# Down layer of the first chunk in fp32, bonus of the second chunk by feature, heads 6/7 of two units by a 0/1 matrix, last down layer by halves

## The chip, the core and the metric

The kernel runs on one core of a Trainium2 chip. The metric is the device time of one execution in microseconds. The engines are TensorE (PE), VectorE (DVE), ScalarE (ACT), GpSimd (POOL) and SyncE (SP), which issues all DMAs here.

## What is computed

A linear attention with decay runs over 4 batches, 8 heads, 768 steps and 48 features; its output of 3072 tokens of 384 features goes through two feed-forward layers. The first takes the largest of three projections and projects down; the second is a gated one. The host of the kernel gives the weights as 64-bit floats.

```python
for t in range(S):
    kt, vt, rt, wt = (k[:, :, t], v[:, :, t], r[:, :, t], w[:, :, t])
    cur = np.einsum('bhd,bhe->bhde', u[None] * kt, vt)
    y[:, :, t] = np.einsum('bhd,bhde->bhe', rt, state + cur)
    state = wt[:, :, :, None] * state + np.einsum('bhd,bhe->bhde', kt, vt)
# first layer, 384 -> 768 -> 384
h = np.maximum(np.maximum(x @ w1, x @ w2), x @ w3);  x = h @ w_out
# second layer, 384 -> 1536 -> 384
g = x @ w_gate;  out = (g * (1.0 / (1.0 + np.exp(-g))) * (x @ w_val)) @ w_out2
```

## The kernel before

**Chunks and units.** The 768 steps are cut into six chunks c = 0 to 5 of 128 steps; a chunk holds 512 tokens (4 batches), which are the columns of its matrices. A chunk's attention is made in four units j, in the order 3, 0, 1, 2, numbered n = 0 to 23 through the kernel. Unit j = 3 makes heads 6 and 7, units 0, 1, 2 two heads each. The matrix x of a chunk has three tiles of 128 rows (k = 0, 1, 2, one for each of units 0, 1, 2): 48 rows of a head, 16 rows of heads 6/7, the same again. The 16-row pieces are copied by small DMAs from the tile of unit 3 (`xsh`, `xsl`) into the tiles of the others (`gather`, L556).

**A unit.** DVE makes a scan of the decays from the end (`suffix`, L358), its product with k (`khats`, L363), a scan from the start (`prefix`, L371) and its product with r (`rps`, L374). PE makes transposes (L461), k-v products (`outer`, L516), scores (L447). The bonus u*r*k stands on the diagonal of the score matrix A: ACT writes A with the bonus (`diag`, L439), DVE masks the scores into it (`causal`, L452). PE adds A times v (`intra`, L476, two halves with a short ACT read, `peek`, between) and the state's part (`inter`, L489) into one PSUM tile `y`. The bonus is made in two ways: in the first chunk DVE multiplies r by k by feature (`rk`, L418), PE sums by u (`rk_sum`, L424), ACT copies (L431); in the others a second copy of r and k, with tokens on partitions (`inpT`, 384 KB), is loaded, POOL multiplies it (`bonus`, L406/407) and DVE sums (`bonus_sum`, L411).

**Two parts.** The large matmuls are made in fp32r with three products: a matrix is an upper part (`hi`, `xh`, `hh`: a copy to fp32r) and a lower part (`lo`, `xl`, `hl`: the rest), and `mm3` (L566 to 569) multiplies upper by upper, upper by lower, lower by upper. So each x, each hidden matrix and each weight needs an ACT copy (`upper` L534, `hidden` L631, `whigh` L596) and a DVE subtraction (`lower` L554, `hidden` L634, `wlow` L599). In the first chunk the lower part of x is made otherwise: PE subtracts the upper part in PSUM by a matrix -1 (`take_upper`, L543), ACT copies the rest (L552). Before that a weight is put together from its 64-bit words by three DVE steps (`f64_bits`, L128 to 130). Weights 0 to 5 are the up weights, 6 and 7 the two halves of the down weights, 8 to 19 those of the second layer.

**First layer.** For each chunk 18 groups `up` (f, m) of nine matmuls of 512 columns, the largest of three m by ACT (m = 0, L624) and DVE (L626), two parts of it; then `down` (m, k) for m = 0, 1, 2 and halves k = 0, 1 of the six f, nine matmuls each. The results go to DRAM (`y1d`). Units of the next chunk are threaded between the groups. After the last unit (`second_half`, L723) the attention's memory is given to the second layer: 72 groups of 27 matmuls.

**Order.** All steps are entered in a table with an engine, a cost, what they wait for and a due time; `Plan.order` (L59) makes the static order of each engine from it. Four PSUM slots (`slot`) are shared by the groups of large matmuls, the transposes, `outer` and the bonus sums; `y` has one tile, which is free when the lower part of the unit before is made.

Of the kernel before, what the change touches and what calls it, by code (L numbers as in the profile page):

```python
# [124 lines left out]
def f64_bits(nc, lw, hw, tmp):  # L125


    yield nc.vector.tensor_scalar(tmp, hw, 3, 0x3FFFFFFF, ALU.logical_shift_left, ALU.bitwise_and)  # L128
    yield nc.vector.scalar_tensor_tensor(lw, lw, 29, tmp, ALU.logical_shift_right, ALU.bitwise_or)
    yield nc.vector.scalar_tensor_tensor(lw, hw, -0x40000000, lw, ALU.bitwise_and, ALU.bitwise_or)  # L130


def f64_general(nc, pool, dst, src):

    n = dst.shape[1]
    for o in range(0, n, 384):
# [5 lines left out]
        list(f64_bits(nc, lw, hw, d.bitcast(I32)))  # L142
# [129 lines left out]
def fused(ctx: ExitStack, tc: tile.TileContext, pk, ub, wt_all, out):  # L272
    nc = tc.nc
    units = [(c, j) for c in range(NC_) for j in ORDER]

# [25 lines left out]
    minus = ap.tile([128, 128], F32R, name="minus")  # L301
    inpA = [ap.tile([128, OFF_KT], F32, name=f"inpA{i}") for i in range(2)]
# [130 lines left out]
    def diag(n, half):  # L433
# [33 lines left out]

    def intra(n, k):

        for b in range(2):  # L470
            for h in range(2):
                for s in range(2):
# [4 lines left out]
                        ys[n][64 * h:64 * h + 64, a, C * b + T * s:C * b + T * s + T],  # L477
                        inpV[n][t, D * i:D * i + 64], A[n][t, i, :],
                        start=(k == 1 and b == 0), stop=True, skip_group_check=True,
# [15 lines left out]
    def first_y(n):  # L495
        ys[n] = psA.tile([128, 2, NT], F32, tag="y", name="y")
        intra(n, 1)
# [87 lines left out]
    def bits(i, k):  # L585

        if k == 0:
            tmp = lp.tile([128, WCH], I32, tag="tmp", name="tmp")
            ops[i] = f64_bits(nc, raws[i][:, :, 0], raws[i][:, :, 1], tmp)
        next(ops[i], None)  # L590

# [29 lines left out]
    def up_out(c, f, m):  # L621
        if m == 0:
# [13 lines left out]
    def down(c, m, k):  # L636
# [3 lines left out]
        for f in range(3 * k, 3 * k + 3):  # L640
            mm3(pss[c, m], hi[6 + k][:, f % 3, q], lo[6 + k][:, f % 3, q], hh[f], hl[f], f == 0, f == 5)
# [114 lines left out]
    for turn, what in enumerate(chunks):  # L756
# [32 lines left out]
        for k in range(3):  # L789
            cost = 0.67 if k == 0 else 1.28  # L790
            war = [L["bits", i - 1, 1]] if k == 0 and ("bits", i - 1, 1) in L else []
            b = L["bits", i, k] = on("DVE", cost, bits, i, k)([ld if k == 0 else b] + war)
        h = L["high", i] = on("ACT", 1.16, whigh, i)([b])
        l = L["low", i] = on("DVE", 1.28, wlow, i)([h], need)
        users[turn] = [l]
# [11 lines left out]
    for n, (c, j) in enumerate(units):  # L807
# [3 lines left out]
        due = 10 + 6.0 * i if early else START[c - 1] + (i + 1) * (PERIOD / 4) - 18  # L811
# [26 lines left out]
        tr = L["tr", n] = on("PE", 0.45, transposes, n)([kh] + prev("outer", n, 1), slot=1, slack=lag)  # L838
# [229 lines left out]
```

## Time and profile before

| | us |
|---|---|
| median of 3 runs (lowest to highest) | 879.13 (878.44 to 879.92) |
| the profiled execution | 879.41 |
| its span, first to last instruction | 877.5 |
| PE busy | 844.8 (96%) |
| DVE busy | 437.5 (50%) |
| ACT busy | 342.5 (39%) |
| POOL busy | 91.1 (10%) |
| mean granted clock of TensorE | 0.982 |

Busy time is a sum over the whole span, and the span has stages with different limits, so the page's strips of 40 slices and tables by stage come first. Matmuls are pipelined: the record of one with 512 columns is 0.39 us long while the next starts 0.23 us later, so a busy PE can still be late. A granted clock of 1.00 is 2.4 GHz, 0.50 is 1.2 GHz. In the first 27 us the column shows 1.00 though the durations of matmuls there are those of the stretches at 0.50.

### The profile page before, as it was taken

Reading aid. Unit: us, or ns where it says so; the run is one execution under the profiler, and the core shown is the slowest. Engines: PE = TensorE matmul, PEld = TensorE weight load, DVE = VectorE, ACT = ScalarE, POOL = GpSimd, SP = SyncE. Lnnn points to the kernel's source line nnn. Section 1 sums busy time; section 2 is a strip of 40 time slices with the busy share of each in tenths; the row PEclk is TensorE's granted clock in tenths of the full one; section 3 lists DMA queues with packets and bytes.
Section 4 is the critical chain, followed back from the end, with each engine's and each line's share of the span. In section 5 each row is a group of like instructions: output and inputs, shape, how many; then the busy total and the mean of one; then the engine's idle time right before and its main releaser. Section 6 shows DMA issues by size and latency. Waiting matters only on the chain.

```text
span 877.5 us, 15085 instructions
## 1 busy us (share of the span) xinstructions
PE 844.8 (96%) x6322; PEld 682.9 (78%) x6322; DVE 437.5 (50%) x626; ACT 342.5 (39%) x721; POOL 91.1 (10%) x116
## 2 busy tenths in 40 slices
PE   6797899999999999989999999999999999999997
PEld 5675677787777778768788888888888888888885
DVE  6999997745665657369884212222222212222221
ACT  4644455655354454455555221232132122222111
POOL 1422133111211100010100100010010010000000
PEclk9699999999999999999999999999999999999999
DMA  8775476355433553154731100020010000000001
GB/s 235 193 211 190 146 226 166 75 171 139 130 94 111 149 133 118 47 186 147 245 112 51 36 37 1 0 72 1 1 36 37 1 13 36 1 1 37 0 1 39
DMA packets 24635, 79.54 MB, mean 91 GB/s; under 512 B 4016, under 2 KB 7216, under 8 KB 20976
## 3 DMA queue, kind: packets, MB, share of 16 engines
q1 hardware_dynamic: 24560, 78.50, 30.0%
q8 instruction: 51, 0.84, 0.4%
q14 instruction: 24, 0.20, 0.1%
HBM read 66.69 MB, written 9.44 MB: 87 GB/s over the span
## 4 chain that ended last, share of the span: by engine, by line
PE 83%; DVE 9%; DMA 4%; ACT 2%; issue 1%; SPq 1%; DVEq 0%
PE ps L567 9%; PE ps L568 9%; PE ps L569 8%; PE po L567 6%; PE po L568 6%; PE pg L568 6%; PE pv L568 6%; PE pg L567 6%; PE pv L567 6%; PE po L569 6%; PE pg L569 6%; PE pv L569 6%; PE y L476 2%; PE sc L447 1%; PE kv L516 1%
## 5 line engine op out<-in xcount | busy, mean ns | idle before, releaser
L696 DVE TENSOR_TENSOR sil<-sil,pv 128x512 f32<-128x512 f32 x72 | 49.4, 686 | 252.1 <-PE pv L569 250.0
L567 PE MATMUL ps<-xh,hi 128*128 128x512 f32 x324 | 133.5, 412 | 4.4 <-DMA xh<-xsh 2.5
L569 PE MATMUL ps<-xh,lo 128*128 128x512 f32 x324 | 129.0, 398 | 1.5 <-DVE lo L599 1.5
L568 PE MATMUL ps<-xl,hi 128*128 128x512 f32 x324 | 128.9, 398 | 1.2 <-DMA xl<-xsl 1.2
L693 ACT ACTIVATE sil<-pg 128x512 f32<-128x512 f32 x72 | 42.9, 596 | 162.3 <-PE pg L569 162.3
L700 ACT ACTIVATE ph<-sil 128x512 fp32r<-128x512 f32 x72 | 45.4, 630 | 126.1 <-DVE sil L696 126.1
L568 PE MATMUL po<-pl,hi 128*128 128x512 f32 x216 | 84.6, 392 | 0.0
L568 PE MATMUL pg<-yl,hi 128*128 128x512 f32 x216 | 84.6, 392 | 0.0
L568 PE MATMUL pv<-yl,hi 128*128 128x512 f32 x216 | 84.6, 392 | 0.0
L567 PE MATMUL po<-ph,hi 128*128 128x512 f32 x216 | 84.5, 391 | 0.0
L567 PE MATMUL pg<-yh,hi 128*128 128x512 f32 x216 | 84.4, 391 | 0.0
L567 PE MATMUL pv<-yh,hi 128*128 128x512 f32 x216 | 84.3, 390 | 0.0
L569 PE MATMUL po<-ph,lo 128*128 128x512 f32 x216 | 83.9, 389 | 0.0
L569 PE MATMUL pg<-yh,lo 128*128 128x512 f32 x216 | 83.9, 389 | 0.0
L569 PE MATMUL pv<-yh,lo 128*128 128x512 f32 x216 | 83.9, 388 | 0.0
L705 DVE TENSOR_TENSOR pl<-sil,ph 128x512 fp32r<-128x512 f32 x72 | 49.8, 691 | 56.7 <-ACT ph L700 56.7
L567 PEld LDWEIGHTS ps<-xh,hi 128*128 128x128 f32 x324 | 62.1, 192 | 20.1 <-issue 2.9
L569 PEld LDWEIGHTS ps<-xh,lo 128*128 128x128 f32 x324 | 62.0, 191 | 16.3 <-DVE lo L599 2.9
L568 PEld LDWEIGHTS ps<-xl,hi 128*128 128x128 f32 x324 | 62.2, 192 | 13.7 <-issue 2.1
L626 DVE TENSOR_TENSOR hw<-hw,ps 128x512 f32<-128x512 f32 x72 | 49.0, 681 | 43.1 <-PE ps L569 36.2
L681 POOL TENSOR_TENSOR yl<-y,yh 128x512 fp32r<-128x512 f32 x18 | 24.2, 1348 | 348.4 <-ACT yh L677 348.4
L439 ACT ACTIVATE A<-stacked,a 128x64 f32<-128x64 f32 x192 | 49.5, 336 | 9.0 <-DVE a L411 8.8
(111 smaller groups left out, 1353.3 us busy)
## 6 DMA issues: line engine op xcount, KB each, us to landing
raw<-wt SPq DMA_DIRECT2D x28, 1152.0 KB, 6.1
inpA<-pk SPq DMA_DIRECT2D x44, 294.0 KB, 5.1
inpT<-pk SPq DMA_DIRECT2D x20, 384.0 KB, 3.8
inpV<-pk SPq DMA_DIRECT2D x24, 200.0 KB, 3.2
y1d<-y1s SPq DMA_DIRECT2D x18, 256.0 KB, 3.2
y<-y1d SPq DMA_DIRECT2D x18, 256.0 KB, 2.6
outT<-os SPq DMA_DIRECT2D x18, 256.0 KB, 2.0
xh<-xsh SPq DMA_DIRECT2D x36, 32.0 KB, 2.6
```

The costliest lines, as they stand in the source:

```text
L439: nc.scalar.activation(A[n][:, i, :], stacked, AF.Copy, scale=sums[n][:, k:k + 1])
L447: nc.tensor.matmul(sc[n][t, a, T * g:T * g + T], khat[n][q, g, t], rp[n % 2][q, g, t], start=True, stop=True)
L476: nc.tensor.matmul(ys[n][64 * h:64 * h + 64, a, C * b + T * s:C * b + T * s + T], inpV[n][t, D * i:D * i + 64], A[n][t, i, :], start=(k == ...
L567: nc.tensor.matmul(ps, lh, rh, start=first, stop=False)
L568: nc.tensor.matmul(ps, lh, rl, start=False, stop=False)
L569: nc.tensor.matmul(ps, ll, rh, start=False, stop=last)
L626: nc.vector.tensor_tensor(hws[f], hws[f], pss[c, f, m], ALU.max)
L681: nc.gpsimd.tensor_tensor(yl[c, m], y1[m], yh[c, m].bitcast(F32), ALU.subtract)
L693: nc.scalar.activation(sil[f % 3], pgs[f % 3, 0], AF.Silu)
L696: nc.vector.tensor_tensor(sil[f % 3], sil[f % 3], pgs[f % 3, 1], ALU.mult)
L700: nc.scalar.activation(h_, sil[f % 3], AF.Copy)
L705: nc.vector.tensor_tensor(l_, sil[f % 3], prod[c, f][0].bitcast(F32), ALU.subtract)
```

## The change

It does six things.

- Units 4 to 7 (the second chunk) make their bonus as the first chunk does: `rk`, `rk_sum`, ACT copy; no `inpT`, no `bonus`, no `bonus_sum`. Their lower parts are made by `take_upper` and ACT; DVE's subtraction goes.
- The first chunk's down layer is 18 fp32 matmuls (whole weight, whole hidden matrix) in place of 54 fp32r ones. The six `hidden` copies and six subtractions of that chunk go; the hidden matrix is kept as it is (`hh`). Weights 6 and 7 are put together into tiles of their own (`whole`) by `f64_bits`, which takes a destination, and their two parts are made behind the first chunk.
- Units 3 and 23 (`LENT`, the last ones of the first and the last chunk) get the rows of heads 6/7 by PE: `lend` multiplies `xsh` and `xsl` by a 0/1 matrix (`shift`, made by ACT at the start) into `y` ahead of `intra`, which then writes 48 rows; their gathers go.
- The last chunk's down layer runs half by half: k = 0 for all three m, then k = 1.
- The costs of PE steps of the first chunk are 1.4 times as large in the planner's table; the last chunk's units are due 12 us earlier.
- A reload of the weights for a check waits for weight 7's third step in place of its lower part.

The core of the diff:

```diff
-def f64_bits(nc, lw, hw, tmp):
+def f64_bits(nc, lw, hw, tmp, dst):
     yield nc.vector.tensor_scalar(tmp, hw, 3, 0x3FFFFFFF, ALU.logical_shift_left, ALU.bitwise_and)
-    yield nc.vector.scalar_tensor_tensor(lw, lw, 29, tmp, ALU.logical_shift_right, ALU.bitwise_or)
-    yield nc.vector.scalar_tensor_tensor(lw, hw, -0x40000000, lw, ALU.bitwise_and, ALU.bitwise_or)
+    yield nc.vector.scalar_tensor_tensor(dst, lw, 29, tmp, ALU.logical_shift_right, ALU.bitwise_or)
+    yield nc.vector.scalar_tensor_tensor(dst, hw, -0x40000000, dst, ALU.bitwise_and, ALU.bitwise_or)
...
+    LENT = (3, 23)
...
     nc.scalar.activation(minus, ident, AF.Copy, scale=-1.0)
+    nc.scalar.activation(shift, minus.bitcast(F32), AF.Copy, scale=0.0)
+    for h in range(2):
+        nc.scalar.activation(shift[:, 64 * h + 48:64 * h + 64], ident[:, 64 * h + 32:64 * h + 48], AF.Copy)
...
+    def lend(n):
+        ys[n] = psA.tile([128, 2, NT], F32, tag="y", name="y")
+        for a in range(2):
+            for k in range(2):
+                nc.tensor.matmul(
+                    ys[n][:, a, 0:2 * C], shift, xs[units[n][0]][k][:, 2 * C * a:2 * C * a + 2 * C],
+                    start=(k == 0), stop=True, skip_group_check=True,
+                )
...
     def bits(i, k):
         if k == 0:
-            tmp = lp.tile([128, WCH], I32, tag="tmp", name="tmp")
-            ops[i] = f64_bits(nc, raws[i][:, :, 0], raws[i][:, :, 1], tmp)
+            lw, hw = raws[i][:, :, 0], raws[i][:, :, 1]
+            if i in (6, 7):
+                whole[i] = lp.tile([128, 3, 384], F32, tag=("wo1l", "tmp")[i - 6], name="whole")
+                t = flat(whole[i]).bitcast(I32)
+                ops[i] = f64_bits(nc, lw, hw, t, t)
+            else:
+                tmp = lp.tile([128, WCH], I32, tag="tmp", name="tmp")
+                ops[i] = f64_bits(nc, lw, hw, tmp, lw)
...
     def up_out(c, f, m):
-        if m == 0:
+        if m == 0 and c == 0:
+            hws[f] = hh[f] = lp.tile([128, NT], F32, tag=f"hh{f}", name="hh")
+            nc.scalar.activation(hws[f], pss[c, f, m], AF.Copy)
+        elif m == 0:
...
         for f in range(3 * k, 3 * k + 3):
+            if c == 0:
+                w = whole[6 + k][:, f % 3, q]
+                nc.tensor.matmul(pss[c, m], w, hh[f], start=(f == 0), stop=(f == 5))
+                continue
             mm3(pss[c, m], hi[6 + k][:, f % 3, q], lo[6 + k][:, f % 3, q], hh[f], hl[f], f == 0, f == 5)
...
+        late = START[1] + 0.75 * PERIOD - 5 if i in (6, 7) else None
+        h = L["high", i] = on("ACT", 1.16, whigh, i)([b], late)
+        l = L["low", i] = on("DVE", 1.28, wlow, i)([h] + ([L["low", 6]] if i == 7 else []), late or need)
...
-        due = 10 + 6.0 * i if early else START[c - 1] + (i + 1) * (PERIOD / 4) - 18
+        cold = 1.4 if early else 1.0
+        due = 10 + 6.0 * i if early else START[c - 1] + (i + 1) * (PERIOD / 4) - (30 if c == 5 else 18)
...
-        if early:
+        if n < 8:
             r = L["rk", n] = on("DVE", 0.61, rk, n)([la] + tw)
-            rs = L["rk_sum", n] = on("PE", 0.3, rk_sum, n)([r], slot=1)
+            rs = L["rk_sum", n] = on("PE", 0.3 * cold, rk_sum, n)([r], slot=1)
...
+        before_y = prev("lower", n, 1)
+        if n in LENT:
+            before_y = [on("PE", 0.8, lend, n)(before_y + L["x", n - 3], slack=lag)]
+        y1_ = L["y1", n] = on("PE", 0.3 * cold, first_y, n)([ca, lv] + before_y, slack=lag)
...
-        if early:
-            tk = on("PE", 0.26, take_upper, n)([u_])
+        if n < 8:
+            tk = on("PE", 0.26 * cold, take_upper, n)([u_])
...
-        if j == 3:
+        if j == 3 or n in LENT:
             L["x", n] = [u_, lw]
...
-            for m in range(3):
+            turns = [(m, k) for m in range(3) for k in range(2)]
+            for m, k in sorted(turns, key=lambda t: t[1]) if c == 5 else turns:
...
+                cost = 2.04 if c else 2.7
+                before = L["down", c, m, k] = on("PE", cost, down, c, m, k)(deps, t0 + 2 * k, slot=int(k == 0))
```

What this makes of the order, at three places. In the rows, `y` is a unit's PSUM tile, `pa` a bonus sum, `kp` transposes, `kv` the k-v products, `sc` scores, `ps` a group of the first layer; lines are those of the kernel that the row is from.

PE in the start, from unit 3's scores on; before:

```order
L447 MATMUL sc<-rp_102,kh 64x64 x16
L516 MATMUL kv<-inpV,khT 64x48 x16
L461 MATMUL kp<-ident,kh 128x128 x4
L476 MATMUL y<-A,inpV 64x64 x16
L489 MATMUL y<-rp_102,s_584 48x64 x8
L447 MATMUL sc<-rp_101,kh 64x64 x16
L543 MATMUL y<-xh,minus 128x256 x2
```

And now:

```order
L452 MATMUL sc<-rp_103,kh 64x64 x16
L478 MATMUL y<-xsh,shift 128x256
L478 MATMUL y<-xsl,shift 128x256
L478 MATMUL y<-xsh,shift 128x256
L478 MATMUL y<-xsl,shift 128x256
L533 MATMUL kv<-inpV,khT 64x48 x16
L429 MATMUL pa<-inpA_93,rk 128x2 x4
L492 MATMUL y<-A,inpV 48x64 x8
L466 MATMUL kp<-ident,kh 128x128 x4
L492 MATMUL y<-A,inpV 48x64 x8
L505 MATMUL y<-rp_103,s_584 48x64 x8
```

The four matmuls of `lend` and unit 4's bonus sum stand ahead of unit 3's `intra`, which is now split by unit 4's transposes.

DVE at the end of the first chunk, until unit 8's first scan (`I`); before:

```order
L626 TENSOR_TENSOR hw<-hw,ps 128x512
L554 TENSOR_TENSOR xl<-y,xh 128x512
L626 TENSOR_TENSOR hw<-hw,ps 128x512
L599 TENSOR_TENSOR lo<-raw,hi 128x1152
L634 TENSOR_TENSOR hl<-hw,hh 128x512
L526 TENSOR_TENSOR S_105<-s_1305,kv 128x192
L634 TENSOR_TENSOR hl<-hw,hh 128x512
L358 SCALAR_TENSOR_TENSOR I<-inpA_92,d1r 128x520
```

And now, with the last three steps of weight 7:

```order
L658 TENSOR_TENSOR hh<-hh,ps 128x512
L457 COPY_PREDICATED A<-mask,sc 128x512
L543 TENSOR_TENSOR s_1275<-s_1274,kv 128x192
L390 TENSOR_TENSOR s_1275<-s_1275,total_100 128x192
L129 SCALAR_TENSOR_TENSOR whole<-raw,whole 128x1152
L658 TENSOR_TENSOR hh<-hh,ps 128x512
L130 SCALAR_TENSOR_TENSOR whole<-raw,whole 128x1152
L543 TENSOR_TENSOR S_106<-s_1275,kv 128x192
L363 SCALAR_TENSOR_TENSOR I<-inpA_93,d1r 128x520
```

The two `hl`, the `xl` and the weight's `lo` are gone from here; the `lo` of weights 6 and 7 stand 15 rows further on, ahead of unit 10's scan and unit 8's mask.

PE at the first chunk's down layer in the changed kernel (18 rows of 128x512 from `hh,hi`, `hl,hi` and `hh,lo` for each m stood here, after all of unit 7's `y`):

```order
L492 MATMUL y<-A,inpV 64x64 x8
L675 MATMUL ps<-hh,whole 128x512 x3
L492 MATMUL y<-A,inpV 64x64 x8
L505 MATMUL y<-rp_103,s_1274 48x64 x8
L505 MATMUL y<-rp_103,s_1275 48x64 x8
L675 MATMUL ps<-hh,whole 128x512 x3
L560 MATMUL y<-xh,minus 128x256 x2
L675 MATMUL ps<-hh,whole 128x512 x12
L466 MATMUL kp<-ident,kh 128x128 x4
```

The first three matmuls of the layer moved into unit 7's `y`, and PE's subtraction of unit 7 between the first and second part.

## Rows read from the trace of the kernel before

**Rows 1.** The page, part 2: busy tenths of DVE in 40 slices

```profile
DVE  6999997745665657369884212222222212222221
```

**Rows 2.** Stages: stretch, length, busy PE PEld DVE ACT POOL, granted clock, DMA share, GB/s

```profile
11.85:45.40 33.55, 26.91 (x560) 23.11 (x561) 30.28 (x44) 19.39 (x60) 9.76 (x12) 0.78 0.78 202
45.40:118.94 73.54, 65.89 (x615) 49.39 (x612) 73.30 (x97) 37.46 (x88) 18.20 (x17) 0.94 0.59 178
85.23:92.06 6.83, 6.14 (x16) 4.25 (x15) 6.83 (x10) 2.53 (x3) 0.64 (x1) 0.50 0.92 318
118.94:372.50 253.56, 252.29 (x2914) 199.67 (x2912) 157.18 (x253) 125.61 (x312) 37.15 (x54) 1.00 0.47 130
...
378.77:382.19 3.42, 3.42 (x10) 2.64 (x9) 0.00 (x0) 1.11 (x3) 1.27 (x1) 0.50 0.97 332
...
427.30:873.70 446.40, 443.97 (x1950) 365.38 (x1948) 125.47 (x175) 125.48 (x209) 15.53 (x12) 1.00 0.09 31
```

**Rows 3.** Timeline of PE: start, length, line, tiles, shapes, count, idle before and releaser

```profile
14.80 1.86 PE L424 MATMUL pa<-inpA,rk 128*128 128x2 f32 x8
...
17.27 0.78 PE L543 MATMUL y<-xsh,minus 128*128 128x256 f32 x2
...
27.39 1.05 PE L424 MATMUL pa<-inpA,rk 128*128 128x2 f32 x8
...
30.29 0.54 PE L543 MATMUL y<-xh,minus 128*128 128x256 f32 x2 [0.26 <-ACT xh L534]
...
36.09 1.11 PE L461 MATMUL kp<-ident,kh 128*128 128x128 f32 x4 [2.08 <-DVE kh L363]
...
54.77 0.60 PE L461 MATMUL kp<-ident,kh 128*128 128x128 f32 x4
55.12 0.48 PE L567 MATMUL ps<-xh,hi 128*128 128x512 f32 x1
```

**Rows 4.** Timeline of DVE in the first chunk

```profile
69.75 0.67 DVE L634 TENSOR_TENSOR hl<-hw,hh 128x512 fp32r<-128x512 f32 x1
70.34 1.35 DVE L599 TENSOR_TENSOR lo<-raw,hi 128x1152 fp32r<-128x1152 f32 x1
71.61 0.75 DVE L128 TENSOR_SCALAR tmp<-raw 128x1152 int32<-128x1152 int32 x1
...
73.55 0.54 DVE L411 TENSOR_REDUCE a<-inpT 128x8 f32<-128x384 f32 x1
74.02 1.23 DVE L371 TENSOR_TENSOR_SCAN F<-inpA,d1f 128x520 f32<-128x520 f32 x1
```

**Rows 5.** Timelines of DVE and POOL, the same time

```profile
36.84 2.03 DVE L371 TENSOR_TENSOR_SCAN F<-inpA,d1f 128x520 f32<-128x520 f32 x1
...
36.57 1.20 POOL L407 TENSOR_TENSOR inpT<-inpT 128x384 f32<-128x384 f32 x1
```

**Rows 6.** Timeline of PE in an up group

```profile
50.01 0.39 PE L567 MATMUL ps<-xh,hi 128*128 128x512 f32 x1
...
50.69 0.39 PE L567 MATMUL ps<-xh,hi 128*128 128x512 f32 x1
```

**Rows 7.** Timelines of PE, ACT and DVE where the last chunk begins

```profile
372.53 0.50 PE L567 MATMUL ps<-xh,hi 128*128 128x512 f32 x1
...
376.65 0.47 PE L567 MATMUL ps<-xh,hi 128*128 128x512 f32 x1 [2.45 <-DMA xh<-xsh]
377.91 0.47 PE L568 MATMUL ps<-xl,hi 128*128 128x512 f32 x1 [0.79 <-DMA xl<-xsl]
...
378.45 0.40 PE L567 MATMUL ps<-xh,hi 128*128 128x512 f32 x1
...
372.67 0.60 ACT L534 ACTIVATE xh<-y 128x512 fp32r<-128x512 f32 x1 [0.27 <-PE y L489]
...
373.30 0.69 DVE L554 TENSOR_TENSOR xl<-y,xh 128x512 fp32r<-128x512 f32 x1 [5.20 <-ACT xh L534]
```

**Rows 8.** Timeline of PE in the last chunk's down layer

```profile
419.18 0.50 PE L568 MATMUL ps<-hl,hi 128*128 128x512 f32 x1 [0.65 <-DVE hl L634]
```

More of the change, by code (lines that the diff above doesn't have):

```diff
@@ L466, in keep @@
         khT[n] = t
+    def lend(n):
[6 more added lines that the diff above has]
+                )
     def intra(n, k):
+        rows = D if n in LENT else 64
         for b in range(2):
@@ L476, in intra @@
                     nc.tensor.matmul(
-                        ys[n][64 * h:64 * h + 64, a, C * b + T * s:C * b + T * s + T],
-                        inpV[n][t, D * i:D * i + 64], A[n][t, i, :],
-                        start=(k == 1 and b == 0), stop=True, skip_group_check=True,
+                        ys[n][64 * h:64 * h + rows, a, C * b + T * s:C * b + T * s + T],
+                        inpV[n][t, D * i:D * i + rows], A[n][t, i, :],
+                        start=(k == 1 and b == 0 and n not in LENT), stop=True, skip_group_check=True,
                     )
@@ L790, in fused @@
             cost = 0.67 if k == 0 else 1.28
[L791 to L795, printed above, removed]
+            war = []
+            if k == 0 and i not in (0, 6):
+                war = [L["bits", 5, 1] if i == 7 else L["low", 7] if i == 8 else L["bits", i - 1, 1]]
+            b = L["bits", i, k] = on("DVE", cost, bits, i, k)([ld if k == 0 else b] + war, need if i in (6, 7) else None)
+        late = START[1] + 0.75 * PERIOD - 5 if i in (6, 7) else None
+        h = L["high", i] = on("ACT", 1.16, whigh, i)([b], late)
+        l = L["low", i] = on("DVE", 1.28, wlow, i)([h] + ([L["low", 6]] if i == 7 else []), late or need)
+        users[turn] = [b if late else l]
         if i >= 8:
@@ L890, in fused @@
                         L["hw", 9 * c + f] = [h1, h2]
-            for m in range(3):
+            turns = [(m, k) for m in range(3) for k in range(2)]
+            for m, k in sorted(turns, key=lambda t: t[1]) if c == 5 else turns:
                 t0 = START[c] + (PERIOD if c < 5 else LAST) * (0.75 + 0.25 * m / 3)
-                for k in range(2):
-                    deps = [before] + [L["hl", c, f] for f in range(3 * k, 3 * k + 3)] + [L["low", 6 + k]]
-                    before = L["down", c, m, k] = on("PE", 2.04, down, c, m, k)(deps, t0 + 2 * k, slot=int(k == 0))
+                deps = [before] + [L["hl", c, f] for f in range(3 * k, 3 * k + 3)]
+                deps.append(L["low", 6 + k] if c else L["bits", 6 + k, 2])
+                cost = 2.04 if c else 2.7
+                before = L["down", c, m, k] = on("PE", cost, down, c, m, k)(deps, t0 + 2 * k, slot=int(k == 0))
+                if c == 0 and m == 2 and k == 0:
+                    L["low", 7]["deps"].append(before)
+                if k == 0:
+                    continue
                 w1 = on("ACT", 0.5, down_out, c, m)([before] + L.get(("hw", 9 * c + 6 + m - 3), []), t0 + 6)
@@ L925, in fused @@
         for m in range(3):
-            war = [L["gather", 21 + q, k] for q in range(3) for k in range(2)]
+            war = [L["gather", 21 + q, k] for q in range(2) for k in range(2)] + [L["y1", 23]]
             if 3 * c + m >= 2:
```

44 lines of the change are left out of this document (26 added, 18 removed).

## The prediction

> **What bounds the kernel now.** I read the page's strip of VectorE (DVE) first [rows 1]: full in slices 2 to 6, some 22 to 130 us, half idle after. TensorE (PE) is busy 96% of the span, an average that hides stages, so the next view is the table by stage [rows 2]. It shows four. From 427.30 to 873.70 the second layer runs: PE 443.97 of 446.40 us, and the change touches nothing there. From 118.94 to 372.50 PE is busy 252.29 of 253.56 us: bound by PE, with no new PE work in it but one small step at its end. From 45.40 to 118.94 (the first chunk's up and down layers, with units 4 to 7 threaded in) DVE is busy 73.30 of 73.54 us while PE shows 7.65 us idle, and 6.83 us of it ran at a granted clock of 0.50, the 1.2 GHz level. From 11.85 to 45.40 (the start) PE is idle 6.64 of 33.55 us and DVE 3.27. So three places can give time: the start, the first chunk, and the seams at 372 and 419 us, which the timelines show [rows 7, 8]. Whatever is saved in one is kept, since what follows is PE work in the same order.
>
> **A step has a price other than its record.** Three matmuls of 512 columns start 0.68 us apart as a group (from 50.01 to 50.69) [rows 6], 0.2275 us each, though each record is 0.39. A PE wait under about 0.16 us is therefore not shown as idle, and a shown one is that much too small. In the first chunk the 216 matmuls of 512 columns need 216 x 0.2275 = 49.1 us; the three units about 3.2 each, 9.6; the half clock costs (6.83 - 0.69) / 2 = 3.1 at 85 us and some 1.1 until 47.7. With 7.65 idle that makes 70.5 of 73.54; I take the missing 3.0 for waits that the records cover. What could vanish if DVE were never last is 7.65 + 3.0 + 3.1 = 13.7 us.
>
> **What DVE loses.** By start-to-start times: four lower parts (the record is that of an `hl`, so 0.59 each [rows 4]), six `hl` (0.59), two `lo` of the down weights (1.27) go from this stretch, 2.4 + 3.5 + 2.5 = 8.4 us; four bonus reductions (0.47) become products r*k (the same shape as an `hl`, 0.59), 0.5 more. Second, DVE gets back time in which GpSimd worked: a scan takes 2.03 us at 36.84, beside a GpSimd product from 36.57 [rows 5], and 1.23 at 74.02 [rows 4]. The GpSimd products of units 4 to 7 go; I count some 4 us of lengthened DVE steps beside them, 3 of these before 45 us. Those of units 8 and 9 stay. So DVE has about 64 us of work where it had 73.3.
>
> **What PE gains in work there.** (1) Down of the first chunk: 18 fp32 matmuls in place of 54. No fp32 matmul of 512 columns is in the trace; one splits into two records (the four of a bonus sum are x8 [rows 3]). Bounds: two records at the cheapest step, 2 x 0.2275 = 0.46 us; or by the fp32 transposes of 128 columns, four of which take 0.35 us to the next start and 0.60 as a record [rows 3], so 2 x 4 x 0.0875 = 0.70 to 2 x 4 x 0.15 = 1.20. I take 0.90, inside the last pair and under its middle because steps overlap: 18 x (0.90 - 0.68) = 3.9 us more; the ends are -4.1 and +9.3. (2) Three bonus sums at 1.0 (27.39: 1.05): 3.0. (3) Four subtractions of the upper part by PE, at most 0.54 a pair [rows 3]: 2.2. (4) In two of the four the pair stands directly behind the `y` matmuls that it follows, so PE, and all up matmuls queued behind, wait for ScalarE's copy of 0.60 [rows 7]: 1.2. Sum 10.3 us.
>
> On (1) the Trainium skill, "FP8 and Floating Point Precision", section TensorE Precision Notes, says that true fp32 takes four passes through the array. At this trace's step that is an estimated 4 x 0.2275 = 0.91 us, and (1) would be 4.1 us; it speaks against this part of the change, three passes being replaced by four, and no run here shows it yet.
>
> So in the first chunk PE needs 73.5 - 13.7 + 10.3 = 70.1 us with no wait left, and becomes the bound, with DVE at 64. DVE is still nine tenths full, so some waits stay: between none and half of the 13.7. I take 2.1 us, nearer none, since DVE has 6 us of slack where it had 0.2. **First chunk: 1.4 us gained** (from 3.4 gained to 3.4 lost, at a price of 0.90).
>
> **The start.** PE gets unit 4's bonus sum (1.86 us at the rate of 14.80 [rows 3]) and four matmuls of 256 columns for unit 3 (two pairs, at most 0.78 each): 3.4 us more. It had 6.64 us idle, the longest wait for DVE, 2.08 at 36.09 [rows 3], and DVE loses 3 us of lengthened steps; unit 1's bonus sum moves into the wait for the first mask. If all idle stays the start is 3.4 us longer, if none, 3.2 shorter; I take 0.5 shorter. The gathers of unit 3 leave SP's queue (four DMAs); the inputs and weights behind them are not what PE or DVE waited for, so nothing is counted.
>
> **Moved.** The `hi` and `lo` of the two down weights go behind the first chunk: 2 x 1.27 us of DVE. Queued behind them is the masking of unit 8's scores. The second of them waits for PE's down (third part, first half); then PE still has three fp32 matmuls, unit 8's transposes and scores and an up group to do (over 5 us) before it needs the mask, DVE the second `lo`, a reduction, a scan and the mask (3.7), and DVE was 157.18 of 253.56 us busy in that stage [rows 2]: nothing counted, 2.5 us lost if the cover fails.
>
> **The seam at 372.5.** Six matmuls of the last chunk's first group run, then PE idles 2.45 and 0.79 us for the gathers of unit 23 [rows 7]; nine steps are 2.05 us, but the next group starts at 378.45 and not 374.58: 3.8 us lost. Then 378.77 to 382.19 is granted 0.50 [rows 2]: another 1.7. With the rows of heads 6/7 already in PSUM, what is late next is ScalarE's copy (372.67 + 0.60) and DVE's subtraction (373.30 + 0.69 = 373.99); the eighth matmul would start at 372.53 + 7 x 0.2275 = 374.12, so nothing waits. The price is two pairs of 256 columns, at most 0.54 each, 1.0 us. **Gain 5.5 - 1.0 = 4.5** (from 2.8, if the clock dips anyway, to 5.0). **The seam at 419.** PE waits 0.65 us shown, 0.8 by steps, for the last `hl` [rows 8]; by halves, three groups stand ahead instead of one. **Gain 0.8** (0 to 0.8).
>
> **Sum.** 0.5 + 1.4 + 4.5 + 0.8 = 7.2 us. The profiled run took 879.41 us (span 877.5), so 872.2; the median of the runs is 0.28 lower, so I say 871.9.
>
> **Rivals.**
> (a) PE takes DVE's place more fully than I think: half of the first chunk's waits stay, since PE now waits for ScalarE copies between its own small steps. First chunk -3.4, start 0, seams 5.3: 1.9 gained, 877.2. For: ten more hand-overs between PE, ScalarE and DVE. Against: DVE's slack. 0.18.
> (b) fp32 at 0.46 to 0.70 us: 3.6 to 8 us more, 868 to 864. The 0.35 us to the next start speaks for it, the 0.60 us record against. 0.10.
> (c) The change at 372 doesn't do what it says: the small matmuls or the copies of unit 23 come late, and the wait goes from a DMA to ScalarE; half of the 5.5 stays: 874.7. 0.09.
> (d) Slower: an fp32 matmul whose weights are not loaded beside the one ahead. A record of two columns in a bonus sum takes 1.05 / 8 = 0.13 us, nearly all of it for weights; on top of 1.20 that is 1.46 us, 18 x 0.56 = 10.1 us more, 882. It turns the sign from 0.90 + 7.2 / 18 = 1.30 us a matmul on. For: nothing else in the trace hides fp32 weights of 128 columns. Against: 512 columns are long beside 0.13 us. 0.07.
> The forecast, 868.5 to 875.5: 0.56.
>
> **How the numbers follow.** The range takes in the forecast, (c), nearly all of (a) and the near end of (b): 866.5 to 877.3. A measurement of this kernel tells about 0.2% from no change, 1.8 us: faster is below 877.4. Faster: the forecast, (b), (c) and half of (a), with something held back for the unknown price: 0.82. Same: the rest of (a), 0.10. Slower: (d) and a little, 0.08.
>
> **What would show it.** In the changed kernel's table by stage: the first chunk's stretch about 72 us with PE nearly without idle and DVE visibly below full; its down matmuls about 0.9 us per fp32 pair of records (1.3 or more is (d)). At the last chunk's start no DMA as releaser and no stretch at 0.50. If the gain is only 2 us with the seam gone, (a) is right. If unit 8's mask comes late, the moved `lo` had no cover. The second layer must take 446 us as before; if it doesn't, something that I have not seen has moved.

## The result and the profile after

| | before | after |
|---|---|---|
| median of 4 runs (lowest to highest), us | 879.52 (878.44 to 881.18) | 867.77 (866.70 to 869.86) |
| the profiled execution; its span, us | 879.41; 877.5 | 868.19; 866.4 |
| PE, DVE, ACT, POOL busy, us | 844.8, 437.5, 342.5, 91.1 | 845.9, 425.5, 340.4, 75.4 |
| mean granted clock of TensorE | 0.982 | 0.994 |

The ratio is 0.9868, 95% interval 0.9843 to 0.9893. The forecast was 871.9 (866.5 to 877.3), faster: the time lies in the range, near its low end. 11.75 us were gained where 7.2 were forecast.

PE is as busy as before; what went is its idle time and its time at half clock. Four places on PE's own path divide the span without a rest:

| stretch on PE | before | after | difference | forecast |
|---|---|---|---|---|
| to the first up matmul | 45.40 | 42.89 | -2.51 | -0.5 |
| from there to the second chunk's first up matmul | 74.92 | 71.04 | -3.88 | -1.4 |
| from there to the last chunk's first up matmul | 252.21 | 252.76 | +0.55 | +1.0 |
| from there to the end | 505.01 | 499.72 | -5.29 | -6.3 |
| sum (the spans) | 877.54 | 866.41 | -11.13 | -7.2 |

The table by stage of the changed kernel answers to [rows 2] (columns as there); the fourth line runs from the last chunk's first up matmul into its down layer:

```profile
11.65:42.89 31.24, 29.33 (x576) 25.58 (x572) 26.59 (x43) 19.08 (x61) 0.95 (x3) 0.90 0.69 177
42.89:112.77 69.88, 66.85 (x630) 48.34 (x627) 68.51 (x89) 37.32 (x92) 15.67 (x17) 1.00 0.65 190
112.77:366.69 253.92, 252.27 (x2918) 199.74 (x2916) 151.63 (x250) 124.66 (x308) 32.41 (x51) 1.00 0.48 130
366.69:421.50 54.81, 54.81 (x247) 45.34 (x242) 46.70 (x46) 30.24 (x43) 8.75 (x6) 1.00 0.49 173
```

In the start PE idles 1.91 of 31.24 us where it idled 6.64 of 33.55, and POOL does 0.95 us where it did 9.76. In the first chunk the granted clock is 1.00 but for its first 0.6 us (0.50 was granted from 36.69 to 43.51), and PE idles 3.03 us where it idled 7.65; but DVE is still busy 68.51 of 69.88. At the last chunk's start and in its down layer PE doesn't idle at all. The page's strip of DVE [rows 1] is no less full in the first chunk than before:

```profile
DVE  7899977546555657379884222222222221212121
```

PE's timeline in the first chunk: a `take_upper` behind the copy that it waits for, a late step of DVE, the last twelve fp32 matmuls (24 records) with what follows, and the wait for unit 8's mask:

```profile
61.08 0.51 PE L560 MATMUL y<-xh,minus 128*128 128x256 f32 x2 [0.72 <-ACT xh L551]
61.42 0.39 PE L584 MATMUL ps<-xh,hi 128*128 128x512 f32 x1
...
72.39 0.69 PE L452 MATMUL sc<-rp,kh 64*64 64x64 f32 x32 [1.25 <-DVE rp L379]
...
102.47 10.46 PE L675 MATMUL ps<-hh,whole 128*128 128x512 f32 x24
112.77 0.60 PE L466 MATMUL kp<-ident,kh 128*128 128x128 f32 x4
...
118.06 0.46 PE L492 MATMUL y<-A,inpV 64*64 64x64 f32 x16 [1.19 <-DVE A L457]
```

Twelve fp32 matmuls take 10.30 us from 102.47 to the next start at 112.77: 0.858 each. The last chunk's first group, which answers to [rows 7], starts its second one 2.18 us behind the first, at full clock (first, eighth and tenth matmul):

```profile
366.69 0.50 PE L584 MATMUL ps<-xh,hi 128*128 128x512 f32 x1
...
368.41 0.39 PE L585 MATMUL ps<-xl,hi 128*128 128x512 f32 x1
...
368.87 0.39 PE L584 MATMUL ps<-xh,hi 128*128 128x512 f32 x1
```

### The profile page after: what moved, and what is told of

It is laid out like the page before. It is cut to its first block, busy times and chain, and to the rows that moved or that the text cites. A ratio compares the mean times of both kernels' runs of the same rounds, so it can differ in the third digit from the quotient of the medians.

```text
span 866.4 us, 15106 instructions
## 1 busy us (share of the span) xinstructions
PE 845.9 (98%) x6352; PEld 683.3 (79%) x6352; DVE 425.5 (49%) x616; ACT 340.4 (39%) x726; POOL 75.4 (9%) x104
## 4 chain that ended last, share of the span: by engine, by line
PE 86%; DVE 8%; ACT 2%; DMA 2%; issue 1%; SPq 0%; DVEq 0%; ACTq 0%
PE ps L584 10%; PE ps L585 9%; PE ps L586 9%; PE po L584 6%; PE po L585 6%; PE po L586 6%; PE pg L584 6%; PE pv L585 6%; PE pg L585 6%; PE pv L584 6%; PE pg L586 5%; PE pv L586 5%; PE y L492 2%; PE sc L452 2%; PE kv L533 1%
## 5 line engine op out<-in xcount | busy, mean ns | idle before, releaser
L584 PE MATMUL ps<-xh,hi 128*128 128x512 f32 x324 | 131.5, 406 | 0.1
L585 PE MATMUL ps<-xl,hi 128*128 128x512 f32 x324 | 126.6, 391 | 0.0
L586 PE MATMUL ps<-xh,lo 128*128 128x512 f32 x324 | 126.6, 391 | 0.0
L658 DVE TENSOR_TENSOR hw<-hw,ps 128x512 f32<-128x512 f32 x60 | 41.0, 683 | 37.4 <-PE ps L586 32.2
```

Of the source, the lines that this page charges most:

```text
L584: nc.tensor.matmul(ps, lh, rh, start=first, stop=False)
L585: nc.tensor.matmul(ps, lh, rl, start=False, stop=False)
L586: nc.tensor.matmul(ps, ll, rh, start=False, stop=last)
L658: nc.vector.tensor_tensor(hws[f], hws[f], pss[c, f, m], ALU.max)
```

## The experiments

All are the changed kernel with one part taken back, but for two that start from the kernel before and one that goes further. Each was timed beside the kernel before, so the ratio (95% interval) is what compares across them. The last column is the first up matmul of the profiled execution and the time from there to the end. The changed kernel's own interval is the widest of the table, and four kernels that take one part back lie within 0.0007 of its ratio: differences of 1 us between rows tell nothing.

| run | median, us (before's beside it) | ratio | first up; rest |
|---|---|---|---|
| before | 879.52 | | 45.40; 832.1 |
| changed kernel | 867.77 (879.52) | 0.9868 (0.9843 to 0.9893) | 42.89; 823.5 |
| lend3only | 866.68 (878.77) | 0.9865 (0.9850 to 0.9880) | 40.24; 823.4 |
| due18 | 866.42 (878.77) | 0.9864 (0.9849 to 0.9879) | 40.71; 822.4 |
| no23_due18 | 870.38 (878.77) | 0.9912 (0.9897 to 0.9928) | 41.18; 825.0 |
| down_3products | 870.54 (878.77) | 0.9899 (0.9884 to 0.9914) | 43.78; 825.5 |
| bonus_gpsimd | 869.08 (878.20) | 0.9903 (0.9888 to 0.9919) | 43.62; 822.9 |
| low47_vector | 867.65 (878.20) | 0.9875 (0.9860 to 0.9890) | 41.51; 825.4 |
| lend23only | 866.73 (878.20) | 0.9871 (0.9856 to 0.9886) | 41.46; 823.4 |
| mask_first | 864.84 (878.20) | 0.9848 (0.9834 to 0.9861) | 40.41; 822.0 |
| before_due30 | 875.21 (878.37) | 0.9963 (0.9950 to 0.9977) | 43.90; 829.1 |
| only_down_fp32 | 876.15 (878.37) | 0.9973 (0.9960 to 0.9986) | 43.91; 828.6 |
| no_halves | 871.81 (878.37) | 0.9919 (0.9905 to 0.9933) | 42.68; 828.5 |
| no_cold | 868.40 (878.37) | 0.9878 (0.9862 to 0.9894) | 41.57; 826.1 |

### What closed the seam at 372 us: the matrix or the due time

The change did two things there: heads 6/7 of unit 23 by PE, and due times 12 us earlier. Three kernels make the square complete.

```diff
-    LENT = (3, 23)
+    LENT = (3,)
```

> The changed kernel with unit 23's rows of heads 6/7 copied by DMAs again (unit 3 keeps the 0/1 matrix; the earlier due time stays). The order now has one group of nine matmuls (2.05 us) between unit 23's last matmul and the last chunk's first up group, where the kernel before had none. My theory (the 0/1 matrix is what removes the seam): the wait of 3.8 us is covered by 2.05 only, some 1.75 us stay, perhaps with a stretch of half clock of 1.7, less the two pairs of `lend` (0.6): 1.1 to 2.9 us more than the changed kernel, 868.9 to 870.7 us, with a PE wait for the gathers at the seam. Rival (the earlier due time alone removes it): no wait there, 867.2 to 867.8 us.

```diff
-... (PERIOD / 4) - (30 if c == 5 else 18)
+... (PERIOD / 4) - 18
```

> The changed kernel with the last chunk's units due as late as before (18 in place of 30 in the table); both units keep the 0/1 matrix. No group stands between unit 23's last matmul and the last chunk's first up group. My theory: the matrix alone is enough, since the eighth matmul starts 1.6 us behind the first and the copy and the subtraction take 1.5: no PE wait over 0.2 us, 867.8 us within 0.6. Rival (the due time is what counts): a wait for ScalarE or VectorE of 1 to 2 us at the seam, 869 to 870 us.

Both edits together:

> The changed kernel with both taken back at the seam: unit 23's rows by DMAs and the due time of before. My theory: the seam is as in the kernel before, PE idle 2.45 and 0.79 us for the gathers and a stretch at half clock behind: 4.5 to 5 us more than the changed kernel, 872.3 to 872.8 us. Rival (the clock does not fall, since the kernel idles less ahead of it): 3.2 us more, 871.0 us.

Measured: 866.68, 866.42 and 870.38 us; the first lies below both numbers that were expected for it. Either part alone does it; only without both is the seam back, at 0.9912 against 0.9864, some 4 us. PE's timeline with neither, then with the due time alone:

```profile
365.15 0.40 PE L586 MATMUL ps<-xh,lo 128*128 128x512 f32 x1
368.01 0.47 PE L584 MATMUL ps<-xh,hi 128*128 128x512 f32 x1 [2.46 <-DMA xh<-xsh]
369.27 0.47 PE L585 MATMUL ps<-xl,hi 128*128 128x512 f32 x1 [0.79 <-DMA xl<-xsl]
```

```profile
365.01 0.47 PE L584 MATMUL ps<-xh,hi 128*128 128x512 f32 x1 [0.45 <-ACT hi L623]
366.29 0.47 PE L585 MATMUL ps<-xl,hi 128*128 128x512 f32 x1 [0.81 <-DMA xl<-xsl]
```

With neither, the waits are those of [rows 7] to 0.01 us, 2.46 and 0.79. With the due time alone, one group of nine matmuls stands between unit 23's last matmul and the first up group, and 1.26 us are left; without `lend`'s own 0.59 us that is about as good as the matrix. My theory held for the matrix, and missed that the due time nearly suffices. In the run with neither, the clock stayed at 1.00 behind the waits, where [rows 2] had 3.42 us at 0.50: in that profile the rival's "no half clock" is what is seen. But that execution took 868.00 us, and the other four took 869.38 to 872.47 at mean granted clocks of 0.984 to 0.990 against its 0.994, so it isn't shown for them. The same date, alone on the kernel before:

> The kernel before with one number changed: the last chunk's units are due 30 ahead in the table in place of 18. One group of nine matmuls then stands between unit 23's last matmul and the last chunk's first up group. Theory, from the run with unit 23's gathers and the early due time: 2.05 of the 3.8 us of the seam are covered, and no or little half clock follows: 2 to 3.7 us less than the kernel before (878.5), 874.8 to 876.5 us. Rival (the seam is worth less without the rest of the change, since the gathers queue behind more transfers): within 1 us of the kernel before.

875.21 us, 3.2 less: one number in the table is worth a quarter of the whole gain.

### The last down layer by halves

```diff
-            for m, k in sorted(turns, key=lambda t: t[1]) if c == 5 else turns:
+            for m, k in turns:
```

> The changed kernel with the last down layer part by part (k = 0, 1 for each m) as before; the order of everything else on TensorE is the same. Theory: the last lower part of the hidden matrix is late again by 0.65 us shown, 0.8 by steps, 0.8 us more than the changed kernel. Rival (the earlier due times and a later VectorE hide it already): no wait there, no difference.

871.81 us, 4.0 more (0.9919 against 0.9868, the intervals apart): five times what the theory had. PE, DVE and POOL in the last down layer:

```profile
410.93 0.50 PE L585 MATMUL ps<-hl,hi 128*128 128x512 f32 x1 [2.88 <-DVE hl L666]
...
406.75 2.44 DVE L130 SCALAR_TENSOR_TENSOR raw<-raw 128x1152 int32<-128x1152 int32 x1
409.11 1.76 DVE L666 TENSOR_TENSOR hl<-hw,hh 128x512 fp32r<-128x512 f32 x1
...
406.69 3.63 POOL L717 TENSOR_TENSOR yl<-y,yh 128x512 fp32r<-128x512 f32 x2 [29.84 <-ACT yh L713]
```

The stretch behind the wait (columns as in [rows 2]):

```profile
411.94:415.35 3.41, 3.41 (x9) 2.63 (x8) 3.38 (x4) 0.88 (x2) 1.27 (x1) 0.50 0.65 183
```

The last lower part is late by 2.88 us where [rows 8] had 0.65, and 3.41 us at half clock follow (1.7 lost). Counted from the last chunk's first up matmul, PE comes to this layer 5.3 us earlier than before (after 36.9 us in place of 42.2), by the seam that is gone; the last `hl` ends only 2.6 us earlier (44.0 in place of 46.6). Between the last maximum and the last `hl` stands now a step of a second-layer weight that takes 2.44 us beside GpSimd, and the `hl` itself takes 1.76. The changed kernel has the same two late steps, and no PE wait: by halves, three groups of work stand ahead of the one that needs this `hl`. DVE and POOL there:

```profile
406.53 2.46 DVE L130 SCALAR_TENSOR_TENSOR raw<-raw 128x1152 int32<-128x1152 int32 x1
408.91 1.79 DVE L666 TENSOR_TENSOR hl<-hw,hh 128x512 fp32r<-128x512 f32 x1
...
406.47 3.69 POOL L717 TENSOR_TENSOR yl<-y,yh 128x512 fp32r<-128x512 f32 x2 [29.80 <-ACT yh L713]
```

So in this order the two edits hang together. From the last chunk's first up matmul to the end: 505.0 us with neither (before), 502.2 by halves alone (no23_due18, its execution of 868.00), 504.4 with the seam closed alone (no_halves), 499.7 with both. Without the halves, nearly all of what the seam gave would have been lost 44 us later. It isn't so in every order: in before_due30, also without the halves, what stands ahead of the last `hl` is a reduction of 1.34 us and the `hl` takes 1.18, PE waits 0.98 us shown, and the stretch is 501.7. The reduction stands there in all kernels in which unit 23 keeps its gathers, the weight step in all that give it the matrix: the later `hl` came with the matrix. No run has the changed kernel with the date alone and without the halves.

### The first chunk's down layer

```diff
         for f in range(3 * k, 3 * k + 3):
-            if c == 0:
+            if False:
                 w = whole[6 + k][:, f % 3, q]
...
-        if m == 0 and c == 0:
+        if False:
             hws[f] = hh[f] = lp.tile([128, NT], F32, tag=f"hh{f}", name="hh")
...
-        late = START[1] + 0.75 * PERIOD - 5 if i in (6, 7) else None
+        late = None
```

> The changed kernel with the first chunk's down layer made of three fp32r products again: 54 matmuls of 512 columns in place of 18 in fp32, six hidden copies on ScalarE and six subtractions on VectorE more, and the two parts of weights 6 and 7 made ahead of it again. TensorE's work falls by 18 x (0.858 - 0.68) = 3.2 us; VectorE's in the first chunk's stretch rises by 6 x 0.59 = 3.5 us from 68.5 of 69.9. Theory A (VectorE is still what sets that stretch, so taking work off it was worth its price on TensorE): the stretch becomes 72 to 74 us, 870 to 872 us in all. Theory B (TensorE sets it): 3.2 us less, and 1.2 less since unit 8's mask is no longer late, 863.4 to 864.6 us.

And the other way round, this part alone on the kernel before:

> Of the change only the first chunk's down layer in fp32 (with the parts of weights 6 and 7 made behind it); bonus, lower parts, gathers, due times, costs and the last down layer as in the kernel before. TensorE's work rises by 18 x (0.858 - 0.68) = 3.2 us, VectorE's in the first chunk's stretch falls by 3.5 to 6.1 us of 73.3. Theory A (VectorE sets that stretch): 2 to 4 us less than the kernel before (878.5), 874.5 to 876.5 us, with the first chunk's stretch some 70 to 72 us. Theory B (the price on TensorE eats it): 0 to 3 us more, 878.5 to 881.5 us.

870.54 us, 2.8 more than the changed kernel (its interval still touches that kernel's, but not those of lend3only and due18); 876.15 us, 2.2 less than the kernel before. Theory A both times, near the forecast numbers. From the first up matmul to the second chunk's, DVE is busy 74.68 of 74.92 us in the kernel before and 71.91 of 71.98 in only_down_fp32. The same stretch in down_3products, then in the changed kernel:

```profile
43.78:117.10 73.32, 67.35 (x685) 53.70 (x681) 72.81 (x95) 41.29 (x99) 14.31 (x14) 0.97 0.58 176
```

```profile
42.89:113.93 71.04, 68.01 (x667) 49.27 (x663) 68.70 (x90) 38.27 (x94) 16.83 (x18) 1.00 0.65 190
```

With three products DVE is full again. PE's busy time hardly tells the kernels apart (67.27, 67.22, 67.35 and 68.01 us in the four), but it holds different amounts of half clock (granted 0.94, 0.97, 0.97 and 1.00) and so doesn't price the work. Cut at the first matmul of the down layer, the stretch shows two limits (length, then busy PE and DVE, us):

| kernel | up to the first down matmul | from it to the second chunk |
|---|---|---|
| before | 59.59, 52.98, 59.35 | 15.33, 14.29, 15.33 |
| only_down_fp32 | 55.27, 50.51, 55.20 | 16.71, 16.71, 16.71 |
| down_3products | 59.44, 53.60, 58.93 | 13.88, 13.75, 13.88 |
| changed kernel | 53.05, 50.02, 52.37 | 17.99, 17.99, 16.33 |

Up to the down layer the length follows DVE, and fp32 makes it 4.3 us shorter on the kernel before and 6.4 on the changed one. From there on PE has no idle time where the layer is in fp32, and its price is paid: 1.4 and 4.1 us longer (1.5 of the 4.1 is unit 7's `y` and `take_upper`, which in the changed kernel fall into this part).

### Bonus and lower parts of the second chunk

```diff
-        if n < 8:
+        if n < 4:
             r = L["rk", n] = on("DVE", 0.61, rk, n)([la] + tw)
```

> The changed kernel (867.8 us; 866.4 in the neighbouring runs) with units 4 to 7's bonus made as before: a second copy of r and k loaded (4 x 384 KB), multiplied by GpSimd, summed by VectorE. TensorE loses four bonus sums (1.05 to 1.86 us in the start, three of some 0.9 in the first chunk), VectorE has four steps of 0.47 in place of four of 0.59. Theory A (the prediction's: VectorE's steps get longer beside GpSimd's, and VectorE is last in both stretches): GpSimd's busy time rises by 17 us, VectorE's steps beside it are longer by some 4 us, and the start or the first chunk gets 1 to 4 us longer: 867.5 to 870.5 us. Theory B (TensorE sets both stretches now, and the bonus by TensorE only costs it): 3 to 4 us less, 863 to 864 us.

869.08 us, 0.9903: 1.3 us more on the medians, 3 by the ratios (the intervals touch here too), and theory A. In the profiled execution the loss is in the start: the first up matmul comes at 43.62, and from there on the kernel needs no more than the changed one (822.9 against 823.5). PE, DVE and POOL there with GpSimd's bonus, then DVE at the same two steps without it (due18, whose order on every engine is that of the changed kernel until ahead of the last chunk):

```profile
34.18 1.12 PE L466 MATMUL kp<-ident,kh 128*128 128x128 f32 x4 [1.18 <-DVE kh L368]
38.09 1.13 PE L452 MATMUL sc<-rp,kh 64*64 64x64 f32 x32 [1.76 <-DVE rp L379]
...
34.31 1.63 DVE L376 TENSOR_TENSOR_SCAN F<-inpA,d1f 128x520 f32<-128x520 f32 x1
36.46 1.48 DVE L379 TENSOR_TENSOR rp<-inpA,F 128x512 f32<-128x512 f32 x1
...
34.21 2.12 POOL L411 TENSOR_TENSOR inpT<-inpT,uB 128x192 f32<-128x192 f32 x2 [0.94 <-DMA inpT<-pk]
```

```profile
33.76 1.23 DVE L376 TENSOR_TENSOR_SCAN F<-inpA,d1f 128x520 f32<-128x520 f32 x1
35.16 0.68 DVE L379 TENSOR_TENSOR rp<-inpA,F 128x512 f32<-128x512 f32 x1
```

Beside GpSimd the scan and the product take 1.2 us more, and the scores wait 1.76 us for that product. How much of the later first up matmul comes from this isn't shown: PE is also granted half the clock from 28.50 to 44.60 us there, and in due18 only from 25.74 to 32.57. The Trainium skill, "SBUF — State Buffer", section Who interferes with whom, says that a VectorE instruction with two inputs in SBUF contends with a GpSimd one that reads SBUF, and that a reduction doesn't. The traces agree: the weight step with two inputs is 1.35 us alone and 2.46 beside `yl` (changed kernel), while the same size's reduction takes 1.34 either way (kernel before, here beside `yl`):

```profile
404.66 1.35 DVE L129 SCALAR_TENSOR_TENSOR raw<-raw,tmp 128x1152 int32<-128x1152 int32 x1
...
416.69 1.34 DVE L603 TENSOR_REDUCE small<-raw 128x1 f32<-128x1152 f32 x1
...
415.38 3.20 POOL L681 TENSOR_TENSOR yl<-y,yh 128x512 fp32r<-128x512 f32 x2 [23.78 <-ACT yh L677]
```

Which step bears it hangs on the order: in low47_vector the weight step begins together with the first `yl` (406.76 and 406.75) and keeps 1.36 us, and the `hl` and a `lo` behind it take 1.80 and 2.44.

The lower parts:

```diff
-        if n < 8:
+        if n < 4:
             tk = on("PE", 0.26 * cold, take_upper, n)([u_])
```

> The changed kernel with the lower parts of units 4 to 7 made by VectorE's subtraction again: four pairs of `take_upper` matmuls (0.24 to 0.5 us each, some 1.5 us) and the waits for ScalarE's copy ahead of two of them (0.72 shown, some 0.85 each) go from TensorE, 4 x 0.59 = 2.4 us come to VectorE, which is 68.5 of 69.9 us busy there. Theory A (VectorE sets the first chunk's stretch): 1 us longer or no change, 867 to 868.8 us. Theory B (TensorE sets it): some 3 us less, 863.5 to 864.8 us.

867.65 us, 0.9875: no difference that the intervals tell. PE is rid of four pairs and two waits, and DVE is 71.15 of 72.33 us busy in the stretch of the table above (71.04 in the changed kernel). Neither engine had the time to spare; this part of the change is worth nothing measurable.

### Unit 3, the planner's costs, and a further version

```diff
-    LENT = (3, 23)
+    LENT = (23,)
```

> The changed kernel with unit 3's rows of heads 6/7 copied by DMAs again (unit 23 keeps the 0/1 matrix). TensorE loses four matmuls of 256 columns ahead of the first up group (1.07 us). Theory A (the kernel before had no wait for unit 3's gathers, so the matrix there bought nothing): 0 to 1 us less, 865.5 to 867.8 us. Theory B (TensorE reaches the first up group 2 to 4 us earlier than before, and now the gathers would be late): a wait for a DMA of 1 to 3 us within the first group, 868 to 870 us.

866.73 us, 0.9871: theory A. The first up group has no wait for a DMA, so the matrix bought nothing for unit 3.

```diff
-        cold = 1.4 if early else 1.0
+        cold = 1.0
```

> The changed kernel with the table's costs of TensorE's steps in the first four units at 1.0 in place of 1.4 times. The same work, in another order until the first up group. Theory (the fill of the start's waits comes from the steps themselves): the first up group starts within 1 us of 40.7 to 42.9, and the time is 867 us within 1. Rival (the order made with the larger costs is what fills the waits): TensorE idles 2 to 4 us more in the start and the time rises by 2 to 3 us.

868.40 us, 0.9878, 0.4 us above the expected range; the first up matmul comes at 41.57, so the start isn't longer, and the difference to the changed kernel isn't told from none. The last one adds to due18:

```diff
-... suffix, n)([la] + prev("kh", n, 1) + prev("total", n, 1))
+... suffix, n)([la] + prev("kh", n, 1) + prev("total", n, 1) + (prev("causal", n, 2) if n == 10 else []))
-            tk = on("PE", 0.26 * cold, take_upper, n)([u_])
+            tk = on("PE", 0.26 * cold, take_upper, n)([u_], slack=0.0 if early else 1.2)
```

> A further version: the changed kernel with the last chunk's units due as late as before (18), unit 8's mask ahead of unit 10's scan on VectorE, and an up group between a unit's last `y` matmul and the `take_upper` behind it for units 4 to 7 (a slack of 1.2 in the table). My theory: the waits of 1.19 us for unit 8's mask and of 0.72 us twice for ScalarE's copies, each some 0.15 longer than shown, are TensorE's own time and vanish: 1.2 to 3 us less than the run with the due time alone (866.4), 863.4 to 865.2 us. Rival (VectorE or ScalarE are late anyway and the wait comes back a step later): no change, 866.4 us within 0.6.

864.84 us, 0.9848: the lowest of all, 1.6 below due18 and 2.9 below the changed kernel, though the intervals still touch. The wait for unit 8's mask is gone, and one of the two for the copies. What came instead, on PE:

```profile
123.89 0.50 PE L584 MATMUL ps<-xh,hi 128*128 128x512 f32 x1 [0.77 <-DVE hw L658]
129.30 0.46 PE L492 MATMUL y<-A,inpV 64*64 64x64 f32 x16 [0.41 <-ACT seen L518]
```

Of some 2 us, 1.2 came back later: theory and rival each have a part.

## Why the prediction was right, and where its sizes were off

The time lies in the range, and each of the four places moved the way that was forecast; yet the two at the front gained 6.4 us where 1.9 were forecast, the first chunk by another path than the one argued. That the total still fits owes something to the width of the range.

**The start: right sign, mis-sized.** The term that failed is "I take 0.5 shorter", between all idle kept and none: 2.5 us went, and 4.7 of the 6.64 us idle, near the end "if none" (3.2). PE's new work took 2.1 us and not 3.4: 1.07 for `lend` (32.35 to 33.42) and 0.99 for the bonus sum (34.03 to 35.02). The reason given, lengthened DVE steps beside GpSimd, has the 1.2 us and the wait in bonus_gpsimd for it. The exact size can't be settled from one profile: due18 has the same order on every engine in the start, and reaches the first up matmul at 40.71 instead of 42.89, with 4.44 us idle from 11.65 on instead of 1.91. A bonus sum and the stretch at half clock, in the changed kernel and then in due18 (stretches with columns as in [rows 2]):

```profile
26.85 1.87 PE L429 MATMUL pa<-inpA,rk 128*128 128x2 f32 x8
...
36.69:43.51 6.82, 6.05 (x164) 5.12 (x156) 5.08 (x9) 5.37 (x13) 0.00 (x0) 0.50 0.22 55
```

```profile
19.00 1.05 PE L429 MATMUL pa<-inpA,rk 128*128 128x2 f32 x8
...
25.74:32.57 6.83, 6.53 (x92) 5.67 (x96) 6.32 (x10) 3.69 (x12) 0.57 (x1) 0.50 0.75 173
```

In the changed kernel's execution the steps are still slow at 26.85 us, in due18's a bonus sum is fast at 19.00. So not all of the idle time that went is gain: slower steps leave less to wait. Six kernels with this order in the start (the changed one, lend3only, due18, no23_due18, mask_first, no_halves) reach the first up matmul at 40.24 to 42.89, the two with the order of before (before, before_due30) at 45.40 and 43.90: 1.0 to 5.2 us gained, more than 0.5 in any pair.

**The first chunk: the price list held, the bound did not.** An fp32 matmul took 0.858 us, 0.90 was taken: 3.2 us in place of 3.9. A bonus sum took 0.81 (49.67 to 50.48), 1.0 taken; a `take_upper` between groups 0.24 (45.34 to 45.58), at most 0.54 taken. The two waits for ScalarE's copies came as forecast, 0.72 shown each (1.2 taken for both). The Trainium skill, "FP8 and Floating Point Precision", section TensorE Precision Notes, gives true fp32 four passes, an estimated 0.91 us at this trace's step; the trace agrees, a little under it. The step that failed is "So in the first chunk PE ... becomes the bound, with DVE at 64": it holds only from the down layer on. Ahead of it DVE is busy 52.37 of 53.05 us, and down_3products shows that giving work back to it costs 2.8 us though PE gets rid of 3.2. The chain that ended last runs there through DVE, and through a weight's load that waits for its buffer (start, length):

```profile
57.66 0.60 DVE hh L658
58.52 0.67 DVE tmp L128
59.19 1.28 DVE lo L628
60.49 7.46 DMA raw<-wt
67.97 0.77 DVE tmp L128
...
69.34 1.15 DVE F L376
70.49 1.25 DVE raw L129
71.74 0.60 DVE rp L379
```

So both counted, one after the other: up to the down layer the stretch is 6.5 us shorter than before (59.59 to 53.05) and follows DVE, from there on 2.7 longer (15.33 to 17.99) and follows PE, 3.9 gained in all. The prediction weighed one sum for PE against one for DVE over the whole stretch. What DVE lost was sized right: 74.68 to 68.70 us between the first two chunks' up matmuls, of which 3.0 are the two `lo`, which I had counted out of it; without them 9.0 went where 9.3 were forecast.

**The moved `lo`: the cover failed, not for the named reason.** "If unit 8's mask comes late, the moved `lo` had no cover" was asked of the trace, and the mask is late by 1.19 us shown (2.5 was the price). DVE ahead of it:

```profile
109.18 3.01 DVE L628 TENSOR_TENSOR lo<-whole,hi 128x1152 fp32r<-128x1152 f32 x2
113.75 0.55 DVE L416 TENSOR_REDUCE a<-inpT 128x8 f32<-128x384 f32 x1 [1.56 <-POOL inpT L412]
116.15 1.24 DVE L363 TENSOR_TENSOR_SCAN I<-inpA,d1r 128x520 f32<-128x520 f32 x1 [1.85 <-DMA inpA<-pk]
117.31 0.70 DVE L457 COPY_PREDICATED A<-mask,sc 128x512 f32<-128x512 uint8 x1
```

Behind the two `lo` DVE stands idle for 1.56 and 1.85 us, for GpSimd's product and for unit 10's inputs, and the mask stands behind both. I had costed the reduction and the scan ahead of the mask by their length alone, without what they themselves wait for. Putting the mask ahead of that scan (mask_first) removed the wait.

**The seams: the sum right, the split wrong.** 6.3 us were forecast in the last stretch, and 1.0 for `lend` ahead of it, which cost 0.59 (360.04 to 360.63). From the last chunk's first up matmul to the second layer's first gate matmul 6.3 went (55.41 to 49.12); 1.0 came back in the second layer's first groups, at a new wait for ScalarE:

```profile
425.00 0.50 PE L584 MATMUL pg<-yh,hi 128*128 128x512 f32 x1 [0.79 <-ACT sil L729]
```

But "gain 4.5" and "gain 0.8" are not two terms. The halves, sized by their wait of before, are worth 4 us in the order that the matrix brought, and in that order the seam is worth next to nothing without them. I asked what is late next at the seam itself, and not at the next place where PE meets DVE.

**The rivals.** (a) has its waits, 1.73 of the 3.03 us idle in the first chunk are for ScalarE (0.72, 0.72, 0.29), but too small: the stretch gained 3.9 where (a) lost 3.4. (c) has no sign, since the seam has no wait. (b) and (d) are settled by the 0.858 us. The second layer, which had to stay as it was, takes 450.6 us from its first gate matmul to the end (415.81 to 866.41), 449.6 before, by the new wait at 425.00.

**Not settled.** Why the clock takes another course in the start from run to run; and how the gain in the start divides between clock and waits.

## What to carry to other kernels

Price a cover in the kernel as it will be, not as it is: once an upstream wait is gone, the next hand-over of the two engines must carry the time that was gained, and an edit worth 0.8 us by its own row can be what keeps 4. When an engine is full in the stretch that counts, work taken off it pays even at a higher price on the engine that looks busier; where the limit passes to the other engine, cut the stretch there and make a sum for each part. And before a new mechanism is built for a late input, try an earlier date: here one number did as much as the matrix, and the last `hl` was less late with it (0.98 us in before_due30, 2.88 in no_halves).

## What the runs showed of the hardware

- An fp32 matmul of 512 columns with 128 x 128 weights took 0.858 us in a row of twelve, below four of the fp32r steps of 0.2275, so no time for its weights is to be seen in it.
- Two VectorE steps of two SBUF inputs beside GpSimd's `yl` took 2.46 in place of 1.35 us and 1.79 in place of 0.69; a reduction of the first one's size was not lengthened (1.34). In low47_vector a step that began together with the first `yl` kept 1.36, and the two behind it took 1.80 and 2.44.
- The same order on all engines met the half clock at 36.69 to 43.51 us in one kernel and at 25.74 to 32.57 in another (the changed kernel, due18), with the first up matmul 2.2 us apart; and the seam's waits of 2.46 and 0.79 us were followed by a stretch at 0.50 in the kernel before and by none in no23_due18.
